# One level of Strassen's algorithm in the second MLP's first product

## The chip, the core and the metric

The kernel runs on one core of a Trainium2 chip, in one launch. The metric is the device time in microseconds (us): the median of three runs.

## The reference

Causal attention with a forget-gate decay over 4 batches of 8 heads (576 rows, head size 64) gives 2304 tokens of 512 features. Two MLPs of 2048 hidden units follow it, each one product into the hidden units, a leaky maximum and one product out of them. The change concerns the second MLP alone, above all its product `x @ w_in`.

```python
def _moe_ref(x, w_in, w_out):            # first MLP
    h = x @ w_in
    g = np.maximum(0.01 * h, h)
    return g @ w_out

def _moe2_ref(x, w_in, w_out, alpha):    # second MLP; alpha: one slope per hidden unit
    h = x @ w_in
    g = np.maximum(h, 0.0) + alpha * np.minimum(h, 0.0)
    return g @ w_out
```

## The kernel before

The engines are TensorE (PE), VectorE (DVE), ScalarE (ACT), GpSimd (POOL) and SyncE (SP), which issues every DMA. Each float32 operand of a big product is carried as two float32r parts, hi + lo, and a product is three matmuls: hi·hi, hi·lo and lo·hi. The tiles are 128 partitions high. A "chunk" is 128 hidden units, so an MLP has 16 chunks (`NF`); each chunk's weights come in two "halves" of 128x512, into the units (half 0) and out of them (half 1).

`Plan` is a list scheduler. Every operation is handed to it (`on`, `plan.op`) with the engine or engines that may take it, an expected time, a due time and the tiles that it touches. Each engine takes the operation that is due first among those whose operands and ring slots are there, and the operations are emitted in the order of these planned starts. So the order on each engine is fixed when the program is built, and at run time each engine goes through its list in order.

The stages lie one after the other:

- Attention of a group of queries (`attention_head`, `attention_scores`, `attention_weights`) is done beside the first MLP's block before the one that needs it.
- The first MLP works in nine blocks of 256 tokens (`T`). `moe_h` computes two chunks of hidden units into one PSUM bank: 2 x 4 x 3 = 24 matmuls with 256 columns. ACT and DVE make the leaky maximum into `gr` and split it into `g` (hi, lo). `moe1_y` adds 24 matmuls to the outputs of each block in two banks (`y`); the outputs go to DRAM (`yd`). 14 of its 32 halves are kept in DRAM once they are converted (`wscr`) and are loaded again in every block (`w_stream`, tiles `ws`); the others stay on chip (tiles `w`).
- The second MLP works in nine blocks of 256 tokens too. `moe2_x` loads a block from `yd` (tile `yraw`) and splits it into `x`. `moe_h` (line 522) makes the units, as before, with the slopes from `nalpha` (ACT lines 536 and 539, DVE line 546). `moe2_y` (line 642) multiplies them out: 6 matmuls with 512 columns per chunk, for two token tiles, added up in two banks.
- `weight` loads a half, which comes as float64, puts a float32 together from its words (one pass of ACT or POOL, three of DVE: lines 453 to 469) and splits it into hi and lo (lines 361 and 366, the helpers' lines `cast` and `sub`). The second MLP's 32 halves are converted from the last block of the first MLP on, and all of them stay on chip.

PSUM has eight banks: two (`y`) hold the blocks' outputs, six (`a`) take everything else.

The lines of a product into the units are

```python
for c in range(c0, c1):
    for i, (a, s) in enumerate(((0, 0), (0, 1), (1, 0))):
        pe.matmul(h()[:, f - f0], lhsT=w.ap[:, a, c * P : (c + 1) * P], rhs=x.ap[:, s, c], ...)
```

Of the kernel before, what the change touches and what calls it, by code (L numbers as in the profile page):

```python
# [19 lines left out]
P = 128  # L20
# [7 lines left out]
PARTS = ((0,), (1,))  # L28
CW = 512
NCV = 2  # L30
NRAW2 = 2
PSG = 0
# [4 lines left out]
NSTREAM = 14  # L37
# [6 lines left out]
NG = 2  # L44
NYSB = 2
W2LEAD = 0
# [16 lines left out]
class Buf:  # L63
    """One tile of a ring; it is allocated when its first operation is emitted."""
# [23 lines left out]
class Plan:  # L88
    """List scheduling: operations are given with engine, expected time, due
    time and the buffers they touch; each engine takes the one that is due  # L90
    first among those whose operands and slots are there. They are emitted in
    the order of their start."""
# [5 lines left out]
    def latency(a, b):  # L98
        """Expected time between the end of an operation and its user's start."""
# [27 lines left out]
    def run(self):  # L127
# [29 lines left out]
        def cost(o, eng, now):  # L157
            """When o would be done on an engine, with a price on the shared ports."""
# [9 lines left out]
        def better(o, eng, now):  # L168
            """Whether no other engine is a better place for o."""
# [13 lines left out]
        while events:  # L183
# [7 lines left out]
            for eng, queue in queues.items():  # L191
                if free.get(eng, 0) > now:
                    continue
                for n in [n for _, n in queue]:
# [17 lines left out]
                    if eng == "pe":  # L212
                        # the array's clock is halved after a tick with few columns
# [31 lines left out]
# Expected times in ns for n columns.  # L245
# [90 lines left out]
    # Due times in ns: the first MLP's blocks of T rows follow the prologue, and  # L336
    # each group's attention is due during the block before the one it belongs to.
# [789 lines left out]
```

## Time and profile before

| | |
|---|---|
| runs | 1044.31, 1044.84, 1046.48 us; median 1044.84 us |
| span of the profiled execution, first to last instruction | 1043.5 us |
| PE busy, matmuls | 1024.1 us, 7466 |
| DVE, ACT, POOL busy | 651.7, 603.6, 85.9 us |
| granted TensorE clock, mean | 0.997 |
| DMA | 166.50 MB, 160 GB/s |

The three runs stand for the time; the profiled execution is a further one, of which the profile shows the span alone. What lies around the span is taken as 1044.84 - 1043.5 = 1.3 us. A row of the profile names a line of the kernel, the engine, the operation and the tiles it writes and reads (out<-in, buffer numbers left out), then how often and how long. The seconds of a matmul's row overlap with its neighbours' (the engine is pipelined), so what a matmul costs is read from the starts of the pieces in the timeline and not from its duration.

### The profile page before, as it was taken

The numbers are of one execution on the slowest core, as the hardware profiler recorded it, in microseconds if no ns is written. First come the engines' busy times: TensorE is split into PE (matmuls) and PEld (weight loads), VectorE is DVE, ScalarE is ACT, GpSimd is POOL, SyncE is SP. The second block draws the span as 40 slices with busy tenths as digits, with TensorE's granted clock in tenths as the row PEclk, the third lists the DMA queues.
The fourth block names the chain that finished last, engine by engine and source line by source line (L and its number), as shares of the span: only waits on it lengthen the run. The fifth ranks groups of instructions, "written<-read, shape, count | busy, mean of one in ns | idle before, by whom it ended". The sixth has DMA issues, their size and how long they took to land.

```text
span 1043.5 us, 20123 instructions
## 1 busy us (share of the span) xinstructions
PE 1024.1 (98%) x7466; PEld 964.6 (92%) x7466; DVE 651.7 (62%) x1837; ACT 603.6 (58%) x1354; POOL 85.9 (8%) x159
## 2 busy tenths in 40 slices
PE   7899999999999999999999999999999999999998
PEld 5698999999999999999999999999999999999997
DVE  7799898888887877788885689423222322322322
ACT  7878787767787877887753456334333323323333
POOL 2000221210121111112010001000000000000000
PEclk9999999999999999999999999999999999999999
DMA  8899898576575665767489783001010100000000
GB/s 268 306 311 325 299 308 290 182 255 222 161 257 190 239 217 166 231 229 235 150 280 321 233 311 102 9 33 41 2 41 1 41 21 21 21 2 21 1 21 21
DMA packets 63234, 166.50 MB, mean 160 GB/s; under 512 B 6592, under 2 KB 20320, under 8 KB 63136
## 3 DMA queue, kind: packets, MB, share of 16 engines
q1 hardware_dynamic: 63136, 165.21, 47.2%
q8 instruction: 59, 0.97, 0.4%
q14 instruction: 39, 0.32, 0.1%
HBM read 148.29 MB, written 16.89 MB: 158 GB/s over the span
## 4 chain that ended last, share of the span: by engine, by line
PE 91%; DMA 6%; DVE 2%; ACT 1%; issue 0%; SPq 0%; ACTq 0%; DVEq 0%
PE bank L522 37%; PE bank L642 19%; PE bank L591 18%; PE bank L881 6%; PE bank L938 5%; PE bank L795 4%; PE bank L785 2%; DMA qk<-qk 2%; DMA vr<-v 1%; DMA ws<-wscr 1%; DMA yraw<-yd 1%; DMA raw<-w 1%; DVE g L366 0%; DVE t L895 0%; DVE cv L469 0%
## 5 line engine op out<-in xcount | busy, mean ns | idle before, releaser
L522 PE MATMUL bank<-x,w 128*128 128x256 f32 x1944 | 257.3, 284 | 0.1
L522 PEld LDWEIGHTS bank<-x,w 128*128 128x128 f32 x1944 | 243.7, 191 | 3.6 <-issue 0.4
L546 DVE SCALAR_TENSOR_TENSOR gr<-gr,nalpha,bank 128x256 f32<-128x256 f32 x144 | 62.8, 477 | 213.1 <-ACT bank L539 213.1
L361 ACT ACTIVATE g<-gr 128x512 fp32r<-128x512 f32 x143 | 90.1, 630 | 86.1 <-DVE gr L546 73.9
L366 DVE TENSOR_TENSOR g<-gr,g 128x512 fp32r<-128x512 f32 x144 | 100.6, 699 | 54.3 <-ACT g L361 53.9
L522 PE MATMUL bank<-x,ws 128*128 128x256 f32 x972 | 132.3, 285 | 1.2 <-DMA ws<-wscr 1.2
L536 ACT ACTIVATE gr<-bank 128x512 f32<-128x512 f32 x72 | 43.1, 598 | 154.7 <-PE bank L522 153.8
L642 PE MATMUL bank<-w,g 128*128 128x512 f32 x540 | 132.1, 391 | 0.0
L522 PEld LDWEIGHTS bank<-x,ws 128*128 128x128 f32 x972 | 123.5, 191 | 3.6 <-DMA ws<-wscr 1.7
L591 PE MATMUL bank<-g,ws 128*128 128x256 f32 x864 | 121.7, 288 | 1.3 <-ACT g L361 1.0
L591 PE MATMUL bank<-g,w 128*128 128x256 f32 x864 | 119.7, 286 | 0.0
L642 PEld LDWEIGHTS bank<-w,g 128*128 128x128 f32 x540 | 99.2, 188 | 19.4
L591 PEld LDWEIGHTS bank<-g,ws 128*128 128x128 f32 x864 | 109.5, 191 | 2.8 <-ACT g L361 1.4
L591 PEld LDWEIGHTS bank<-g,w 128*128 128x128 f32 x864 | 109.1, 191 | 0.4 <-issue 0.2
L906 ACT ACTIVATE t<-t,nm 128x128 f32<-128x128 f32 (+4 forms) x160 | 92.6, 580 | 17.2 <-DVE nm L895 16.6
L921 ACT ACTIVATE t<-t,nm 128x128 f32<-128x128 f32 (+4 forms) x139 | 78.2, 574 | 18.9 <-DVE nm L767 17.5
L858 POOL TENSOR_SCALAR_AFFINE_SELECT dm<-cb 128x128 f32<-128x128 f32 (+2 forms) x120 | 59.3, 496 | 358.3 <-DVE nm L895 274.9
L361 ACT ACTIVATE pt<-bank 128x128 fp32r<-128x128 f32 (+4 forms) x189 | 72.0, 408 | 25.9 <-PE bank L938 24.4
L938 PE MATMUL bank<-ident,t 128*128 128x128 f32 (+1 forms) x480 | 73.5, 269 | 1.5 <-ACT t L921 1.3
L952 DVE TENSOR_TENSOR pt<-bank,pt 128x128 fp32r<-128x128 f32 (+1 forms) x144 | 62.4, 452 | 11.7 <-ACT pt L361 10.3
L522 PE MATMUL bank<-x,v 128*128 128x256 f32 x540 | 69.6, 283 | 0.0
L522 PEld LDWEIGHTS bank<-x,v 128*128 128x128 f32 x540 | 68.1, 192 | 1.5
(98 smaller groups left out, 1407.6 us busy)
## 6 DMA issues: line engine op xcount, KB each, us to landing
ws<-wscr SPq DMA_DIRECT2D x112, 512.0 KB, 4.5
raw<-w SPq DMA_DIRECT2D x64, 512.0 KB, 6.3
qk<-qk SPq DMA_DIRECT2D x32, 416.0 KB, 4.4
qk<-qk SPq DMA_DIRECT2D x32, 320.0 KB, 4.5
cb<-cum_d SPq DMA_DIRECT2D x32, 288.0 KB, 4.4
vr<-v SPq DMA_DIRECT2D x16, 480.0 KB, 4.9
wscr<-ws SPq DMA_DIRECT2D x14, 512.0 KB, 5.7
cb<-cum_d SPq DMA_DIRECT2D x31, 160.0 KB, 4.2
```

The lines of the kernel that those rows point to most:

```text
L361: act.activation(out=out, in_=in_, func=AF.Copy)
L366: (dve if e == "dve" else gps).tensor_tensor(out=out, in0=in0, in1=in1, op=ALU.subtract)
L522: pe.matmul(h()[:, f - f0], lhsT=w.ap[:, a, c * P : (c + 1) * P], rhs=x.ap[:, s, c], start=c == 0 and i == 0, stop=c == NC - 1 and i == 2,)
L546: dve.scalar_tensor_tensor(out=gr.ap[:, i], in0=gr.ap[:, i], scalar=nalpha[:, f0 + i : f0 + i + 1], in1=h()[:, i], op0=ALU.mult, op1=ALU.add,)
L591: pe.matmul(acc[c // 2].ap[:, c % 2 * T :][:, :T], lhsT=w.ap[:, a, col : col + P], rhs=g.ap[:, s, at : at + T], start=f == 0 and (a, s) == ...
L642: pe.matmul(acc[t].ap, lhsT=g.ap[:, s, at + t * P : at + (t + 1) * P], rhs=w.ap[:, a], start=f == 0 and (a, s) == (0, 0), stop=f == NF - 1 ...
L858: gps.affine_select(out=dm.ap[:, : nk - split], in_=cb.ap[:, split:nk], pattern=[[-1, nk - split]], compare_op=ALU.is_ge, fill=-MASKED / S ...
L881: pe.matmul(sp_.ap[:, : s1 - s0], lhsT=q.ap[:, ql : ql + P], rhs=k, start=j == 0, stop=j == len(ks) - 1 and not masked,)
L906: act.activation(out=t.ap[:, :nk], in_=t.ap[:, :nk], func=AF.Exp, scale=-1.0, bias=nm.ap[:, last, u : u + 1], accum_out=nm.ap[:, 2, u : u ...
L921: act.activation(out=t.ap[:, :nk], in_=t.ap[:, :nk], func=AF.Copy, scale=nm.ap[:, 3, u : u + 1])
L938: pe.transpose(tp.ap[:, (j - j0) * nq : (j - j0 + 1) * nq], t.ap[p0:, k0 : k0 + P], ident[p0:, p0:])
L952: dve.tensor_tensor(out=lo, in0=src, in1=f32(hi), op=ALU.subtract)
```

## The change

The second MLP's product into the units is done by Strassen's algorithm (Winograd's form of it, 7 products and 15 sums), one level. The two by two blocks are: hidden units in two halves (chunk p and chunk p + 8, a "pair"), features in two halves of 256, tokens in two halves of 384 (`N2`). So the second MLP has three blocks of 768 tokens (`T2`) of eight pairs each.

- `weight2_in` converts both chunks' half 0 of a pair, forms the sums of weights (`comb`, four passes of 256 columns) and splits 3.5 tiles of 128x512 (`stage`), which go to DRAM (`w2in`). Pairs 2 to 5 are due during the first MLP's blocks 3 to 6 and are staged in tiles of the ring `g`, which now has three and is taken in any order; pairs 6, 7, 0 and 1 follow late in the first MLP. Pairs 0 and 1 stay on chip for the first block (tiles `wa`, `ws`); every other use loads the tiles from DRAM (`w2_stream`, up to 512 KB each).
- `moe2_x` loads 768 tokens in two parts (two of the four feature chunks each, tile `yraw`, of which there is one), forms four sums per part and splits seven operands.
- `moe2_h` does seven products per pair, each 6 matmuls with 384 columns into one bank of the ring `y`. ACT copies the first out, DVE adds the other six up in seven sums (`add`, line 720, reading PSUM) into four quarters, and makes the leaky maximum (lines 740 and 743) and the split of each quarter.
- `moe2_y` multiplies each quarter out: nine matmuls with 512 columns, into six banks of the ring `a`, which hold the block's outputs.
- The out halves (`weight2_out`) are converted from the end of the first MLP on, into the tiles `w` as they come free. The first MLP keeps 16 halves in DRAM instead of 14.

```diff
-NCV = 2
-NRAW2 = 2
+NCV = 3
-NSTREAM = 14
+NSTREAM = 16
-NG = 2
+NG = 3
...
+    T2 = 768
+    N2, NP, NB2 = T2 // 2, NF // 2, NT // T2
...
+        def stage(src, cols, k, n):
+            t = new(tag)
+            split_w(src, cols, t, d, n)
+            on("dma", t_dma(8 * n * P), d + 2e3, lambda: sp.dma_start(
+                out=w2in[p, k, :, :, :n], in_=f32(t.ap[:, :, :n])), r=[t], a=[(w2_b, (p, k))])
+            ts.append(t)
...
+        stage(v1, lambda: f32(v1.ap), 0, CW)
+        comb(s3, a11, a21, ALU.subtract, [v1, v2], [(sc, 0)])
+        comb(a21, a21, a22, ALU.add, [], [v2])
+        stage(v2, lambda: f32(v2.ap), 1, CW)
+        comb(s2, a21, a11, ALU.subtract, [v1, v2], [(sc, 1)])
+        stage(sc, lambda: flat(sc.ap), 2, CW)
+        comb(a12, a12, s2, ALU.subtract, [(sc, 1)], [v1])
+        stage(v1, a12, 3, h)
...
+    PRODUCTS = ((0, 0), (2, 1), (0, 1), (2, 0), (1, 0), (1, 1), (3, 0))
...
+        def product(k):
+            b = new("a" if early else "y")
+            t, o = ts[PRODUCTS[k][0]], PRODUCTS[k][1] * (CW // 2)
+
             def fn():
+                for c in range(2):
+                    for i, (a, s) in enumerate(((0, 0), (0, 1), (1, 0))):
                         pe.matmul(
+                            b.ap[:, :N2], lhsT=t.ap[:, a, o + c * P : o + (c + 1) * P], rhs=view(k)[:, s, c],
+                            start=c == 0 and i == 0, stop=c == 1 and i == 2,
                         )
...
+        p1, u2, u3, c22 = (new("r") for _ in range(4))
+        b = product(0)
+        on("act", t_act(N2) - 40, d - URGENT, lambda b=b: act.activation(out=p1.ap, in_=b.ap[:, :N2], func=AF.Copy), r=[b], w=[p1])
+        b = product(1)
+        add(1, u2, b, p1)
+        b = product(2)
+        add(2, p1, b, p1)
+        leaky(p1, 2, 0, 0)
...
+        b = product(6)
+        add(6, u2, b, u2)
+        leaky(u2, 6, 0, 1)
```

How the lists of two engines change is shown at two places. In the names, `x`, `bx` and `by` are the token operands, `wa` and `ws` the weight sums, `g` and `g2` the split units, `w`, `v` the halves of weights, `cv` and `raw` the conversion's tiles; the second number of a name only counts tiles.

PE in the middle of the second MLP, before: two chunks' products (line 522) and outputs (line 642).

```order
L522 MATMUL bank3_69<-x_1_9876,w9_1_0_8954 128x256 x12
L522 MATMUL bank3_69<-x_1_9876,ws_3_8963 128x256 x12
L522 MATMUL bank4_70<-x_1_9876,ws_1_9050 128x256 x6
L642 MATMUL bank0_66<-w7_0_0_8779,g_0_10877 128x512 x2
L642 MATMUL bank1_67<-w7_0_0_8779,g_0_10877 128x512 x2
L642 MATMUL bank0_66<-w7_0_0_8779,g_0_10877 128x512
```

PE at the same stage now, in the last block:

```order
L711 MATMUL bank0_69<-by_2_11293,ws_2_11904 128x384 x6
L780 MATMUL bank6_75<-w_8_9448,g2_0_12038 128x512 x2
L780 MATMUL bank4_73<-w_8_9448,g2_0_12038 128x512 x2
L780 MATMUL bank2_71<-w_8_9448,g2_0_12038 128x512 x2
L780 MATMUL bank6_75<-w_8_9448,g2_0_12038 128x512
L780 MATMUL bank4_73<-w_8_9448,g2_0_12038 128x512
L780 MATMUL bank2_71<-w_8_9448,g2_0_12038 128x512
L711 MATMUL bank1_70<-bx_3_10414,wa_0_11954 128x384 x6
L780 MATMUL bank5_74<-w_10_9571,g_1_12084 128x512 x2
L780 MATMUL bank3_72<-w_10_9571,g_1_12084 128x512 x2
L780 MATMUL bank7_76<-w_10_9571,g_1_12084 128x512 x2
L711 MATMUL bank0_69<-x_0_10479,wa_2_12011 128x384 x6
```

Blocks of 12 matmuls with 256 columns gave way to single products of 6 with 384, and between two of them stand six or nine matmuls of outputs; the units `g_1_12084` that are multiplied out behind line 711's second row come from the product in the first row.

PE where the first MLP ends, before (line 591 is its output, lines 522 and 642 are the second MLP's):

```order
L522 MATMUL bank3_69<-x_0_7973,v4_0_7823 128x256 x12
L591 MATMUL bank0_66<-g_1_9132,ws_2_8924 128x256 x4
L591 MATMUL bank1_67<-g_1_9132,ws_2_8924 128x256 x4
L591 MATMUL bank0_66<-g_1_9132,ws_2_8924 128x256 x2
L591 MATMUL bank1_67<-g_1_9132,ws_2_8924 128x256 x2
L591 MATMUL bank0_66<-g_1_9132,w15_1_0_1807 128x256 x4
```

PE there now (line 612 is the first MLP's output):

```order
L612 MATMUL bank0_69<-g_0_9222,w_15_1628 128x256 x2
L612 MATMUL bank1_70<-g_0_9222,w_15_1628 128x256 x2
L711 MATMUL bank4_73<-bx_0_8655,wa_0_8320 128x384 x6
L711 MATMUL bank3_72<-bx_2_8726,wa_0_8320 128x384 x6
L711 MATMUL bank2_71<-x_2_9191,wa_3_8443 128x384 x6
L711 MATMUL bank0_69<-bx_0_8655,ws_1_9133 128x384 x6
L711 MATMUL bank5_74<-bx_1_8717,wa_2_8433 128x384 x6
L711 MATMUL bank7_76<-bx_3_8735,wa_2_8433 128x384 x6
L711 MATMUL bank6_75<-x_0_8691,wa_1_8339 128x384 x6
L711 MATMUL bank4_73<-x_1_8779,wa_1_8339 128x384 x6
L711 MATMUL bank1_70<-bx_1_8717,ws_3_9219 128x384 x6
L780 MATMUL bank5_74<-w_0_8822,g_1_9377 128x512 x2
```

Before, products of the second MLP stood between the first's last outputs; now they stand behind all of them, nine products in a row.

DVE at that place, before (line 546 makes the second MLP's units, the other rows convert weights and split):

```order
L366 TENSOR_TENSOR g_1_9132<-gr_1_9089,g_1_9132 128x512
L463 SCALAR_TENSOR_TENSOR cv2_0_9015<-raw2_0_8965,cv2_0_9015 128x512
L546 SCALAR_TENSOR_TENSOR gr_0_9116<-gr_0_9116,nalpha_78,bank6_72 128x256 x2
L469 SCALAR_TENSOR_TENSOR cv2_0_9015<-raw2_0_8965,cv2_0_9015 128x512
L366 TENSOR_TENSOR g_0_9172<-gr_0_9116,g_0_9172 128x512
```

DVE there now (`yraw_0_9217` is the second part of the tokens):

```order
L382 TENSOR_TENSOR bx_0_8655<-yraw_0_9217,bx_0_8655 128x384
L382 TENSOR_TENSOR x_2_9191<-yraw_0_9217,x_2_9191 128x384
L382 TENSOR_TENSOR bx_2_8726<-yraw_0_9217,bx_2_8726 128x384
L382 TENSOR_TENSOR yraw_0_9217<-yraw_0_9217 128x384
L472 SCALAR_TENSOR_TENSOR cv_0_9224<-raw_3_9049,cv_0_9224 128x512
L382 TENSOR_TENSOR xt_0_9297<-yraw_0_9217 128x384
L382 TENSOR_TENSOR x_0_8691<-yraw_0_9217,x_0_8691 128x384
L382 TENSOR_TENSOR yraw_0_9217<-yraw_0_9217 128x384
L382 TENSOR_TENSOR bx_1_8717<-xt_0_9297,bx_1_8717 128x384
L382 TENSOR_TENSOR yraw_0_9217<-yraw_0_9217,xt_0_9297 128x384
L382 TENSOR_TENSOR bx_3_8735<-yraw_0_9217,bx_3_8735 128x384
L382 TENSOR_TENSOR w_6_9306<-cv_0_9224,w_6_9306 128x512
```

All of the second part's sums and splits now stand where PE wants the first products' operands, mixed with conversions.

## Rows read from the trace of the kernel before

**Rows 1.** The page: busy time, share of the span and instructions of each engine.

```profile
PE 1024.1 (98%) x7466; PEld 964.6 (92%) x7466; DVE 651.7 (62%) x1837; ACT 603.6 (58%) x1354; POOL 85.9 (8%) x159
```

**Rows 2.** The chain that ended last, shares of the span by line.

```profile
PE bank L522 37%; PE bank L642 19%; PE bank L591 18%; PE bank L881 6%; PE bank L938 5%; PE bank L795 4%; PE bank L785 2%; DMA qk<-qk 2%; DMA vr<-v 1%; DMA ws<-wscr 1%; DMA yraw<-yd 1%; DMA raw<-w 1%; DVE g L366 0%; DVE t L895 0%; DVE cv L469 0%
```

**Rows 3.** Stretches: length, each engine's busy time, granted clock, DMA share, GB/s.

```profile
25.00:170.00 145.00, 138.71 (x998) 126.84 (x998) 128.30 (x409) 115.94 (x291) 19.29 (x32) 1.00 0.91 310
170.00:450.00 280.00, 279.96 (x2305) 275.12 (x2302) 226.68 (x769) 214.27 (x533) 42.47 (x86) 1.00 0.66 217
450.00:520.00 70.00, 70.00 (x578) 69.28 (x579) 61.27 (x186) 55.97 (x127) 11.52 (x20) 1.00 0.58 197
...
590.00:660.00 70.00, 68.85 (x529) 66.50 (x528) 56.48 (x101) 38.02 (x67) 3.00 (x2) 1.00 0.56 195
660.00:1000.00 340.00, 340.00 (x2186) 310.68 (x2186) 104.11 (x201) 116.12 (x207) 0.00 (x0) 1.00 0.07 21
```

**Rows 4.** PE in order of time, from 916 us: start, length, line, operation, count.

```profile
916.30 5.20 PE L522 MATMUL bank<-x,w 128*128 128x256 f32 x42
921.34 1.55 PE L642 MATMUL bank<-v,g 128*128 128x512 f32 x6
922.72 1.52 PE L642 MATMUL bank<-w,g 128*128 128x512 f32 x6
924.08 0.88 PE L522 MATMUL bank<-x,w 128*128 128x256 f32 x6
924.80 2.91 PE L642 MATMUL bank<-w,g 128*128 128x512 f32 x12
927.54 2.68 PE L522 MATMUL bank<-x,w 128*128 128x256 f32 x21
```

**Rows 5.** PE's groups by shape: count, busy us, mean ns of one, idle before.

```profile
L642 PE MATMUL bank<-w,g 128*128 128x512 f32 x540 | 132.1, 391 | 0.0
...
L591 PE MATMUL bank<-g,w 128*128 128x256 f32 x864 | 119.7, 286 | 0.0
...
L881 PE MATMUL bank<-k 128*128 128x384 f32 x24 | 8.1, 338 | 0.0
```

**Rows 6.** What PE waited for: us in total, times, longest us.

```profile
PE bank L881 <- DMA qk<-qk: 7.3, 4, 4.4
...
PE bank L881 <- DVE nm L895: 1.0, 1, 1.0
PE bank L591 <- DVE g L366: 0.3, 1, 0.3
```

**Rows 7.** DVE in order of time at 471 us and 639 us, back to back.

```profile
470.76 0.68 DVE L366 TENSOR_TENSOR g<-gr,g 128x512 fp32r<-128x512 f32 x1
471.36 0.68 DVE L952 TENSOR_TENSOR pt<-bank,pt 128x512 fp32r<-128x512 f32 x1
471.96 0.60 DVE L895 CUSTOM_DVE_ANT_0 t<-bank,dm 128x448 f32<-128x448 f32 x1
...
639.01 0.75 DVE L460 TENSOR_SCALAR cv<-cv 128x512 int32<-128x512 int32 x2
```

**Rows 8.** All engines in order of time at the end of the span.

```profile
1033.71 0.59 ACT L539 ACTIVATE bank<-bank 128x512 f32<-128x512 f32 x1
...
1034.33 0.87 DVE L546 SCALAR_TENSOR_TENSOR gr<-gr,nalpha,bank 128x256 f32<-128x256 f32 x2 [0.56 <-ACT bank L539]
1035.30 0.63 ACT L361 ACTIVATE g<-gr 128x512 fp32r<-128x512 f32 x1 [1.00 <-DVE gr L546]
1035.96 0.69 DVE L366 TENSOR_TENSOR g<-gr,g 128x512 fp32r<-128x512 f32 x1 [0.76 <-ACT g L361]
...
1038.81 1.21 ACT L361 ACTIVATE ysb<-bank 128x256 f32<-128x256 f32 x4 [2.88 <-PE bank L642]
```

**Rows 9.** DMA issues: count, KB each, median us to landing.

```profile
ws<-wscr SPq DMA_DIRECT2D x112, 512.0 KB, 4.5
...
wscr<-ws SPq DMA_DIRECT2D x14, 512.0 KB, 5.7
...
yraw<-yd SPq DMA_DIRECT2D x9, 512.0 KB, 3.8
```

More of the change, by code (lines that the diff above doesn't have):

```diff
@@ L43 @@
 NGR = 2
-NG = 2
+NG = 3
 NYSB = 2
-W2LEAD = 0
+W2LEAD = 60e3
+NEARLY = 4
+W2FROM = 3
+W2EACH = 1
+W2LAG = 50e3
+W2STEP = 8e3
+W2OUT = 15e3
+AHEAD2 = 25e3
+NR = 8
+NG2 = 5
 NBC = 1
@@ L339, in tile_forgetting_attention_two_moe @@
     start, span, now = [], [], PROLOGUE
-    for i in range(2 * NB):
+    for i in range(NB):
         start.append(now)
@@ L420, in tile_forgetting_attention_two_moe @@
+    for b, ap in ((ident_b, ident), (warm_b, warm), (alpha_b, alpha), (cum_b, cum_d), (yd_b, yd), (wscr_b, wscr), (w2_b, w2in), (rate_b, rate), (tri_b, tri)):
         b.ap = ap
-    w_t = {}
-    def slot(which, f, half):
-        if which:
-            i = 2 * f + half
-            return f"v{i}" if i < NP2 else SLOTS2[i - NP2]
-        return "ws" if (f, half) in STREAM else f"w{f}_{half}"
-    SLOTS2 = [slot(0, *w) for w in HALVES if w not in STREAM[:-NSTR]]
-    NP2 = len(HALVES) - len(SLOTS2)
@@ L439, in weight, with assemble @@
-    def weight(which, f, halves, d):
-        n, at = 512 * len(halves), 512 * halves[0]
-        tag = "2" if which and f % 2 else ""
-        raw, v = new("raw" + tag), new("cv" + tag)
-        src = (w1, w2)[which].bitcast(I32)[f, :, 2 * at : 2 * (at + n)]
-        ts = [new(slot(which, f, half)) for half in halves]
+    w_t, w2_t = {}, {}
+    def assemble(which, f, half, d, after=()):
+        raw, v = new("raw"), new("cv")
+        src = (w1, w2)[which].bitcast(I32)[f, :, 2 * CW * half : 2 * CW * (half + 1)]
@@ L494, in w_stream @@
     def w_stream(f, half, d):
-        t = w_t[0, f, half] = new(slot(0, f, half))
+        t = w_t[0, f, half] = new("ws")
         on("dma", t_dma(4096 * P), d, lambda: sp.dma_start(out=f32(t.ap), in_=wscr[f, half]),
                 r=[(wscr_b, (f, half))], w=[t])
-    x_t = {}
+    x_t, begun = {}, {}
     URGENT = 8e3
@@ new lines, in product, with add, split, hi @@
+            on("pe", t_mm(N2, 6), d + k * step, fn, r=[t, bt[k]], w=[b], after=[begun[NB - 1, NF - 2]])
+            return b
+        def add(k, out, b, x):
+            on("dve", t_dve(N2), d + k * step - URGENT, lambda: dve.tensor_tensor(
+                out=out.ap, in0=b.ap[:, :N2], in1=x.ap, op=ALU.add), r=[b] if x is out else [b, x], w=[out])
+        def split(c, k, i, j):
+            g = new(("g", "g2", "g", "g")[2 * i + j])
+            u = d + k * step - URGENT
+            def hi(e):
+                cast(e, g.ap[:, 0, :N2], c.ap)
+            def lo(e):
+                sub(e, g.ap[:, 1, :N2], c.ap, f32(g.ap[:, 0, :N2]))
+            plan.op(t_cast(N2), u, hi, r=[c], w=[(g, "hi")], shared=True)
+            plan.op(t_sub(N2), u, lo, r=[c, (g, "hi")], w=[(g, "lo")], shared=True)
+            gs[i, j] = g
@@ new lines, in moe2_h @@
+        gs = {}
+        p1, u2, u3, c22 = (new("r") for _ in range(4))
[6 more added lines that the diff above has]
+        leaky(p1, 2, 0, 0)
+        b = product(3)
+        add(3, u3, b, u2)
+        b = product(4)
+        add(4, c22, b, u3)
+        add(4, u2, b, u2)
+        leaky(c22, 4, 1, 1)
@@ new lines, in moe2_h, with moe2_y, mm, fn @@
+        b = product(5)
+        add(5, u3, b, u3)
+        leaky(u3, 5, 1, 0)
+        b = product(6)
+        add(6, u2, b, u2)
+        leaky(u2, 6, 0, 1)
+        return gs
+    def moe2_y(bi, p, ts, gs, acc):
+        t0, d = bi * T2, due2(bi, p + 1)
+        quarters = ((0, 0), (1, 1), (1, 0), (0, 1))
+        for k, (i, j) in enumerate(quarters):
+            w, g = w_t[1, p + NP * i, 1], gs[i, j]
+            for t in range(N2 // P):
+                def mm(s, t=t, i=i, j=j, w=w, g=g):
+                    def fn():
+                        for a in range(2 - s):
+                            pe.matmul(
+                                acc[j * (N2 // P) + t].ap, lhsT=g.ap[:, s, t * P : (t + 1) * P], rhs=w.ap[:, a],
+                                start=p == 0 and i == j and (a, s) == (0, 0), stop=p == NP - 1 and i != j and s == 1,
+                            )
+                    return fn
+                at = d + PAIR / 14 * (2 * k + 1 if p < NP - 1 else 7 + j * (N2 // P) + t)
+                on("pe", t_mm(512, 2), at, mm(0), r=[w, (g, "hi")], w=[acc[j * (N2 // P) + t]])
+                on("pe", t_mm(512), at + 1, mm(1), r=[w, (g, "lo")], w=[acc[j * (N2 // P) + t]])
+        if p == NP - 1:
+            halves = 2 if bi == NB2 - 1 else 1
+            m = DM // halves
+            for t in range(T2 // P):
@@ L1028, in tile_forgetting_attention_two_moe @@
     for f in range(NF):
-        for halves in PARTS:
-            weight(0, f, halves, due(0, f) - 10e3 + 1e3 * halves[0])
+        for half in range(2):
+            weight1(f, half, due(0, f) - 10e3 + 1e3 * half)
     for bi in range(NB):
@@ L1057, in tile_forgetting_attention_two_moe, with reopen, fn @@
-    ring("cv2", NRAW2, [P, CW], I32, pool="p2", after=opened)
-    d0, d1 = start[NB - 1] - W2LEAD, start[NB] + 0.3 * span[NB]
-    for f in range(NF):
-        for halves in PARTS:
-            weight(1, f, halves, d0 + (d1 - d0) * (2 * f + halves[0]) / len(HALVES))
-    for bi in range(NB, 2 * NB):
-        moe2_x(bi)
-        acc = [new("y") for _ in range(T // P)]
-        for f in range(0, NF, 2):
-            g = moe_h(bi, f)
-            for i in range(2):
-                moe2_y(bi, f + i, g, acc)
+    def reopen(ctx2, name, side):
+        def fn():
+            ctx2.close()
+            pools[name] = ctx.enter_context(tc.tile_pool(name=name, bufs=1, side=side))
+        return fn
```

249 lines of the change are left out of this document (149 added, 100 removed).

## The prediction

> **What bounds the kernel now.** I read the busy shares first: PE is at work for 1024.1 of 1043.5 us and no other engine for more than 62% [rows 1]. The chain that ended last is mostly three lines of matmuls, the second MLP's 522 and 642 among them [rows 2]. Then I cut the span into its stages. From 660 to 1000 us, the second MLP alone, PE is busy in 340.00 of 340 us at full clock, DVE in 31% and ACT in 34%, and DMA is nearly idle [rows 3]. From 170 to 520 us, the first MLP with attention beside it, PE is full too, but DVE is at 81 to 88% [rows 3]. So matmul time taken out of the second MLP comes out of the end one for one, as long as DVE, which takes over the sums, keeps up; and work that is moved ahead goes to a stage with little DVE time left.
>
> **Price of a matmul.** Six pieces of the steady stage give it by their starts [rows 4]: 42 matmuls with 256 columns from 916.30 to 921.34, 0.120 us each; 12 with 512 columns from 924.80 to 927.54, 0.228 us each. The difference is 0.42 ns per column, and 12 ns of each matmul do not depend on its width. No long run of 384 columns stands in the trace. In a line between the two it costs 0.174 us. In favour of the line: the durations of single ones, 286 ns at 256 columns, 338 at 384 and 391 at 512, lie on one [rows 5]. Ends: 0.180 (the rate of 256 columns) and 0.171 (the rate of 512).
>
> **Removed and added on PE.** Before: 9 blocks x 16 chunks x 12 = 1728 matmuls with 256 columns, 207.4 us. After: 3 blocks x 8 pairs x 7 products x 6 = 1008 with 384 columns, 175.4 us. That is 32.0 us less: 23 us from an eighth of the columns, 9 us from 720 fewer fixed parts. With the ends of the price: 26 to 35 us less. The outputs keep their 864 matmuls with 512 columns. A pair now takes 42 x 0.174 + 36 x 0.228 = 15.5 us of PE.
>
> The Trainium skill (TensorE: Matmul & The Clock Gate, section Back-to-back issue gap) gives a lone matmul's gap as the columns at 2.4 GHz plus about 2.5 ns, which would make 109 and 163 ns and, as an estimate, a gain of 24.9 us. The measured 120 and 228 ns do not agree with it, and the sum goes by them.
>
> **What DVE takes over.** Back to back, a 512-column pass with two operands takes 0.60 us, start to start [rows 7]; two passes of 256 take 0.87 [rows 8], so 384 columns lie between 0.44 and 0.60, and I take 0.52. A pass with one operand took 0.75 for two of 512 [rows 7], some 0.27 for 384. A pair needs seven sums, four halves of a maximum at 0.52 and four at 0.27, four lo parts: 3.6 + 3.2 + 2.1 = 8.9 us, beside 15.5 us of PE. In the mean that is hidden. ACT loses the two passes per bank (lines 536, 539) and gets five short ones; it is freer than before.
>
> What could fail is the delay. Between the product that completes the first quarter and the matmuls that use it the order puts one product and nine matmuls of outputs: 1.04 + 9 x 0.228 = 3.1 us. The chain there is sum, minimum, maximum, hi part: 0.52 + 0.27 + 0.52 + 0.5 = 1.8 us, with four hand-overs of 0.03 to 0.1 us as at the end of the span [rows 8], so 2.2 us. 0.9 us are left for another pass that is ahead on DVE, and such a pass is 0.5 us. I take no loss in the steady stage.
>
> **The first MLP's stage.** A pair's sums of weights cost DVE two conversions (0.38 + 0.60 + 0.60 each), three and a half lo parts and four sums of 256 columns: 3.2 + 2.2 + 1.7 = 7.1 us. Four pairs are moved into four blocks of about 70 us, in which DVE was busy for 57 and, in the last, 61 us [rows 3]: now 64 to 68 of 70. A stage of that kind stands in the trace: from 25 to 170 us DVE is busy 88%, and PE stands for 6.3 of 145 us; but most of this is waiting for loads of q and k, and DVE is named for 1.0 us [rows 6]. So the ends are 0 (450 to 520 us, 88% and no idle time) and 4.3% of 280 us, 12 us. Add to it the staging. Each staged tile is stored before its slot is free, a store of this size lands after 5.7 us [rows 9], and at 14 of the 24 staged tiles of pairs 2 to 7 the next writer of the slot stands only 3 to 5 us of PE behind the store; ACT, which casts, then stands for a microsecond or two with everything behind it. PE has a bank or two of work ahead, so I take 5 us for the whole stage, nearer to 450-520 us, and 0 to 14 as ends. Two more halves in DRAM are two more loads of 4.5 us landing per block [rows 9], 10 us ahead: nothing.
>
> **Where the MLPs meet.** Before, products of the second MLP filled the first's last gaps, and PE stood for 1.15 us between 590 and 660 [rows 3]. Now the first MLP's last outputs wait for their own units, whose chain has conversions in it: 0.6 us. Then come nine products (9.4 us), and DVE must split the second part of the tokens for them, which cannot be loaded before the first part has left the one tile `yraw`. The order has 30 DVE passes from the last units' maximum to the first quarter's: ten of 0.60, two of 0.38, sixteen of 0.52, one of 0.44, one of 0.27, together 15.8 us, begun some 2.2 us before PE ends the outputs of the units before the last. PE needs 2.9 + 9.4 = 12.3 us in that stretch. DVE ends at 13.6, the cast adds 0.5, so 1.8 us are lost; the load is half as large again as the one that lands in 3.8 us [rows 9] and costs about 0.8 more. Conversions of the out halves (2.2 us each, two per pair) fill DVE to 13.3 of 15.5 us per pair through this block; I add 1.3 us. Together 4.5 us, less the 1.15 that stood there: 3.4 us, ends 0 and 9.
>
> **Block changes and end.** Twice the next block's tokens are split in the last pair's time, with `yraw` again loaded in sequence: 0.5 us each, 1 us, ends 0 and 4. Streaming 3.5 tiles per pair is 1.8 MB in 15.5 us, 118 GB/s, where 310 GB/s were moved from 25 to 170 us [rows 3], and each tile is loaded a pair ahead: hidden; uncovered, a tile would cost its 4.5 us. After the last matmul, four copies and a store remain as before [rows 8]: nothing.
>
> **The sum.** Span 1043.5 - 32.0 + 5 + 3.4 + 1 = 1020.9; with 1.3 us around it, as the median stands to the span, 1022 us. The ends of the terms that are likely together give 1015 to 1028.
>
> **Rivals.**
>
> *Little is lost:* the order covers the conversions and the meeting as well as 450 to 520 us were covered. Then 1044.8 - 32 and 0 to 2 us: 1013. For it: PE had no idle time at 88% DVE [rows 3]. Against: the nine products in a row.
>
> *The first MLP's stage is crowded:* DVE full and ACT behind the staging stores cost 12 to 16 us instead of 5: 1029 to 1033. For it: 97% DVE in the last of these blocks. Against: PE's rows name DVE for 1.3 us in the whole span [rows 6].
>
> *The quarters come late:* every pair has four gates, a quarter's chain against the matmuls that use it, 96 in all, and PE goes through its list in order. If DVE's list puts passes of a neighbouring quarter ahead, the 0.9 us of room are gone, and each tenth of a microsecond of lateness costs 9.6 us. From 0.27 us per gate on the kernel is slower than before; at 0.35 it takes 1022 + 34 = 1056 us. For it: seven dependent sums per pair, where before one chain per two chunks had six banks of room, and now two banks. Against: 57% DVE, and an engine that falls behind by one pass catches up in the next gap.
>
> *The wider matmul saves no fixed part:* 384 columns cost 0.180 us, gain 26 us: 1028. The page of the skill named above would give a gain of this size (24.9 us, 1029).
>
> *The change doesn't do what it says:* the weights' tiles come late from DRAM, because SP's list is in order and a load behind a store that waits for its tile waits too. 22 pairs at 0.6 us each would give 13 us: 1035.
>
> **How the numbers follow.** Forecast (1015 to 1028) 0.62; crowded stage 0.14; little lost 0.10; late quarters 0.05; no fixed part saved 0.03; late tiles 0.03; more than one of these 0.03. The predicted time is 1022 us. The range 1011 to 1033 holds the forecast, little lost, no fixed part saved and most of the crowded stage, 0.86; I keep it, since the prices of the delays are estimates. A measurement of this kernel can tell 0.2%, 2.1 us, from no change. Slower by more needs late quarters at their price: 0.05. Within 0.2%: 0.02. Faster: 0.93.
>
> **What would show it.** Products of 6 matmuls 1.04 us apart from start to start (1.08: the fixed part). DVE at 55 to 60% in the second MLP, and PE there without idle time; if PE is named waiting for `g` on ACT or DVE in each pair, the quarters are late. From 270 to 490 us PE idle 2 to 8 us, ACT waiting for DMA on `g`. Where line 711 begins, PE idle 3 to 6 us, released by ACT or DVE rows on `bx`, `x` and `g`. I am wrong if PE is at less than 97% from 650 us on.

## The result, and the profile after

The changed kernel takes 1032.5 us (median of 4 runs, 1028.8 to 1037.2), the kernel before in the same comparison 1044.6 (1043.6 to 1046.5): ratio 0.9875, interval 0.9839 to 0.9911. It is 12.0 us faster, where 22.6 were forecast. The profiled execution has a span of 1029.6 us and took 1031.4, so 1.8 us lie around the span and not the 1.3 that were taken from two different executions.

First the busy shares, then the stretches of [rows 3] (columns: PE, weight loads, DVE, ACT, POOL, granted clock, DMA share, GB/s):

```profile
PE 999.5 (97%) x6746; PEld 936.6 (91%) x6746; DVE 794.3 (77%) x2166; ACT 565.6 (55%) x1311; POOL 82.1 (8%) x156
```

```profile
25.00:170.00 145.00, 133.02 (x912) 120.15 (x913) 119.51 (x368) 108.05 (x264) 13.41 (x23) 0.96 0.83 284
170.00:450.00 280.00, 277.88 (x2279) 272.47 (x2280) 237.75 (x795) 217.16 (x539) 50.16 (x93) 1.00 0.76 254
450.00:520.00 70.00, 69.30 (x566) 67.88 (x565) 63.51 (x199) 58.48 (x136) 12.85 (x23) 1.00 0.88 298
590.00:660.00 70.00, 67.73 (x528) 66.43 (x527) 54.42 (x102) 34.89 (x64) 0.00 (x0) 1.00 0.92 314
660.00:1000.00 340.00, 340.00 (x1697) 306.85 (x1696) 241.17 (x499) 84.13 (x163) 1.02 (x1) 1.00 0.42 138
```

The last row is the stage the change is about: PE full, DVE at 71% instead of 31%. The four rows above it are stages in which time was to be lost. The least expected is the first: PE is busy for 133.0 of the 145 us in which it was busy for 138.7 before, and the granted clock fell to 0.96.

PE in order of time where the MLPs meet (start, length, line, operation, count; in brackets idle time and what ended it):

```profile
644.62 1.70 PE L612 MATMUL bank<-g,ws 128*128 128x256 f32 x12 [1.24 <-ACT g L377]
...
648.64 1.66 PE L711 MATMUL bank<-bx,wa 128*128 128x384 f32 x8 [0.19 <-DVE bx L382]
...
652.22 2.24 PE L711 MATMUL bank<-bx,wa 128*128 128x384 f32 x12
654.30 2.24 PE L711 MATMUL bank<-x,wa 128*128 128x384 f32 x12
...
658.37 1.89 PE L780 MATMUL bank<-w,g 128*128 128x512 f32 x7 [0.78 <-ACT g L377]
```

12 matmuls with 384 columns lie between 652.22 and 654.30: 0.173 us each, a product 1.04 us. The three waits sum to 2.2 us. The passes that DVE took over, in the same stretch (back to back, so the cost is start to start):

```profile
651.47 0.55 DVE L382 TENSOR_TENSOR yraw<-yraw 128x384 f32<-128x384 f32 x1
651.94 0.55 DVE L382 TENSOR_TENSOR bx<-xt,bx 128x384 fp32r<-128x384 f32 x1
...
658.14 0.41 DVE L740 TENSOR_SCALAR gr<-r,alpha 128x384 f32<-128x384 f32 x1
658.47 0.56 DVE L720 TENSOR_TENSOR r<-bank,r 128x384 f32<-128x384 f32 x1
658.93 0.56 DVE L382 TENSOR_TENSOR g<-r,g 128x384 fp32r<-128x384 f32 x1
```

A sum of 384 columns takes 0.47 us, from on-chip memory or from PSUM, and a pass with one operand 0.33.

What PE waited for in the first 170 us (us in total, times, longest):

```profile
PE bank L925 <- DMA vr<-v: 5.8, 2, 3.1
PE bank L1021 <- DMA qk<-qk: 4.9, 2, 4.2
PE bank L1078 <- ACT t L1061: 3.4, 5, 1.6
PE bank L564 <- DMA ws<-wscr: 2.8, 1, 2.8
```

Beside [rows 6], the loads of `v` cost more, and a streamed half of weights is waited for, which did not occur before. The row of `v` in the same stretch of the kernel before:

```profile
PE bank L785 <- DMA vr<-v: 2.5, 3, 1.4
```

### The profile page after: what moved, and what is told of

Same layout as the page of the kernel before. It is cut to its first block, busy times and chain, and to the rows that moved or that the text cites. A ratio compares the mean times of both kernels' runs of the same rounds, so it can differ in the third digit from the quotient of the medians.

```text
span 1029.6 us, 19383 instructions
## 1 busy us (share of the span) xinstructions
PE 999.5 (97%) x6746; PEld 936.6 (91%) x6746; DVE 794.3 (77%) x2166; ACT 565.6 (55%) x1311; POOL 82.1 (8%) x156
## 4 chain that ended last, share of the span: by engine, by line
PE 81%; DMA 10%; DVE 5%; ACT 2%; issue 1%; SPq 0%; ACTq 0%; DVEq 0%
PE bank L780 19%; PE bank L612 16%; PE bank L711 16%; PE bank L564 16%; PE bank L1021 4%; PE bank L1078 4%; DMA raw<-w 4%; PE bank L935 3%; DMA vr<-v 3%; PE bank L925 2%; DMA ws<-wscr 2%; DMA w2in<-g 1%; DVE cv L467 1%; DVE t L1035 1%; DVE cv L472 0%
## 5 line engine op out<-in xcount | busy, mean ns | idle before, releaser
L780 PE MATMUL bank<-w,g 128*128 128x512 f32 x864 | 223.3, 392 | 0.8 <-ACT g L377 0.8
L780 PEld LDWEIGHTS bank<-w,g 128*128 128x128 f32 x864 | 160.2, 188 | 24.3 <-ACT g L377 1.1
L720 DVE TENSOR_TENSOR r<-bank,r 128x384 f32<-128x384 f32 x168 | 91.2, 555 | 77.9 <-PE bank L711 77.2
L564 PE MATMUL bank<-x,w 128*128 128x256 f32 x972 | 136.6, 287 | 0.5 <-ACT x L377 0.3
L564 PEld LDWEIGHTS bank<-x,w 128*128 128x128 f32 x972 | 123.6, 191 | 2.1 <-DVE x L382 0.6
L1046 ACT ACTIVATE t<-t,nm 128x128 f32<-128x128 f32 (+4 forms) x160 | 92.5, 579 | 16.2 <-DVE nm L1035 15.4
L1061 ACT ACTIVATE t<-t,nm 128x448 f32<-128x448 f32 (+4 forms) x140 | 79.2, 577 | 15.8 <-DVE nm L907 14.1
L377 ACT ACTIVATE pt<-bank 128x128 fp32r<-128x128 f32 (+5 forms) x190 | 72.4, 407 | 22.8 <-PE bank L1078 21.4
L382 DVE TENSOR_TENSOR g<-r,g 128x384 fp32r<-128x384 f32 x96 | 53.9, 561 | 22.1 <-ACT g L377 22.1
L1078 PEld LDWEIGHTS bank<-ident,t 128*128 128x128 f32 (+1 forms) x480 | 52.9, 142 | 13.7 <-ACT t L1061 7.1
```

The lines of the kernel that those rows point to most:

```text
L377: act.activation(out=out, in_=in_, func=AF.Copy)
L382: (dve if e == "dve" else gps).tensor_tensor(out=out, in0=in0, in1=in1, op=ALU.subtract)
L720: on("dve", t_dve(N2), d + k * step - URGENT, lambda: dve.tensor_tensor(out=out.ap, in0=b.ap[:, :N2], in1=x.ap, op=ALU.add), r=[b] if x is ...
L780: pe.matmul(acc[j * (N2 // P) + t].ap, lhsT=g.ap[:, s, t * P : (t + 1) * P], rhs=w.ap[:, a], start=p == 0 and i == j and (a, s) == (0, 0), ...
L1046: act.activation(out=t.ap[:, :nk], in_=t.ap[:, :nk], func=AF.Exp, scale=-1.0, bias=nm.ap[:, last, u : u + 1], accum_out=nm.ap[:, 2, u : u ...
L1061: act.activation(out=t.ap[:, :nk], in_=t.ap[:, :nk], func=AF.Copy, scale=nm.ap[:, 3, u : u + 1])
```

## The experiments

Four theories for the missing 10 us; A to C have the letters that the expectations give them. **A**: the choice of the streamed halves. With 16 halves of the first MLP in DRAM instead of 14, block 1 needs halves into the units early, and PE waits for their loads. **B**: the conversions that were moved into blocks 3 to 6 cost more than 5 us. **C**: any new setting, the three tiles `cv` for conversions instead of two (`NCV`) too, gives the first two blocks another order, in which loads come late by chance. **D**: the second MLP does not gain what was forecast, for instance because each quarter is late.

All kernels are in one table; busy and span are of the profiled execution, idle is their difference, "first 170" is PE's busy time there. A single execution lies up to 6.4 us off the median of its kernel's runs, and the kernel before took 1044.6 to 1045.7 us beside the different groups of runs, so sizes go by the ratios and places by the spans.

| kernel | us | ratio to before, interval | span | PE busy | idle | first 170 |
|---|---|---|---|---|---|---|
| before | 1044.6 | | 1043.5 | 1024.1 | 19.4 | 157.7 |
| before, 15 halves | 1048.3 | 1.0038 [1.0022, 1.0053] | 1047.2 | 1026.6 | 20.6 | 157.5 |
| before, 16 halves | 1051.7 | 1.0056 [1.0034, 1.0078] | 1051.2 | 1027.2 | 24.0 | 155.6 |
| before, 18 halves | 1050.7 | 1.0054 [1.0038, 1.0071] | 1051.7 | 1026.5 | 25.2 | 152.7 |
| before, 16 halves, NCV 3 | 1057.5 | 1.0123 [1.0105, 1.0140] | 1055.7 | 1030.6 | 25.1 | 152.4 |
| **changed** | 1032.5 | 0.9875 [0.9839, 0.9911] | 1029.6 | 999.5 | 30.1 | 150.8 |
| changed, out halves streamed | 1032.8 | 0.9861 [0.9837, 0.9886] | 1030.4 | 1003.1 | 27.3 | 155.0 |
| changed, no early pairs | 1042.0 | 0.9964 [0.9942, 0.9985] | 1039.3 | 1004.9 | 34.4 | 153.2 |
| changed, NCV 2 | 1028.8 | 0.9815 [0.9786, 0.9843] | 1023.4 | 998.0 | 25.4 | 156.5 |
| changed, four loads | 1032.2 | 0.9872 [0.9854, 0.9890] | 1028.4 | 999.9 | 28.5 | 150.9 |
| changed, dear quarters (one run) | 1033.2 | | 1031.4 | 1001.5 | 29.9 | 151.7 |
| changed, NCV 2, four loads | 1020.0 | 0.9769 [0.9744, 0.9794] | 1016.4 | 995.4 | 21.0 | 157.0 |
| changed, NCV 2, four loads, out halves | 1018.3 | 0.9737 [0.9709, 0.9766] | 1016.2 | 995.9 | 20.3 | 157.6 |

### 16 halves in the kernel before

```diff
-NSTREAM = 14
+NSTREAM = 16
```

> The kernel before, with 16 of the first MLP's halves kept in DRAM instead of 14, picked as the changed kernel picks them; nothing else. In the changed kernel PE was busy 150.8 us of the first 170, before 157.7, and lost some 3 us more at half clock. Theory A (the loss is made by which halves are streamed: with 16, halves into the units are among the first that block 1 needs, and PE waits for them): 1049 to 1055 us, about 5 to 10 more than before, with PE waiting for ws from wscr at the start of the second block. Theory B (the loss is made by the conversions that were moved into blocks 3 to 6): 1043 to 1047, as before. Theory C (any new setting makes the planner order the first two blocks anew, and how late SP's loads come there is chance): anywhere from 1040 to 1052, with waits on loads of q, k, v in the first 170 us, not on ws above all.

It costs some 6 us, and the products have nothing to do with it. PE's row for the first 170 us, of the kernel before and of this one (PE busy, granted clock, DMA share, GB/s):

```profile
0.00:170.00 170.00, 157.70 (x1078) 0.99 0.90 304
```

```profile
0.00:170.00 170.00, 155.62 (x1050) 0.99 0.90 304
```

Of the 4.6 us more of idle time 2.1 lie here; the rest is spread up to 590 us. No streamed half is waited for in the first 170 us; what is longer than before are waits for ACT and for loads of `v`. The time lies in the ranges of A and of C, the missing wait speaks for C, and B, which expected no change here, does not explain these 6 us.

### 16 other halves in the changed kernel

```diff
-    STREAM = [HALVES[1 + i * (len(HALVES) - 4) // (NSTREAM - 1)] for i in range(NSTREAM)]
+    STREAM = [(f, 1) for f in range(NF)]
```

> The changed kernel, with the 16 halves out of the units streamed and all halves into them kept on chip. Theory A: the wait of 2.8 us on ws near 137 us and the stretch at half clock behind it go: 1024 to 1028 us. Theory B: 1030 to 1036, no change. Theory C: the first two blocks are ordered anew, 1022 to 1037.

The total stays, where A expected 1024 to 1028 us. The wait on `ws` is gone, the first 170 us gain 4 us of PE and 170 to 520 us 2. But where the MLPs meet PE now loses 4.7 us in two waits for ACT, and the same matmuls are busy for 3.6 us more in sum:

```profile
645.35 2.80 PE L711 MATMUL bank<-bx,wa 128*128 128x384 f32 x9 [2.93 <-ACT bx L377]
658.20 2.34 PE L780 MATMUL bank<-w,g 128*128 128x512 f32 x9 [1.75 <-ACT g L377]
```

So the same number of halves can be streamed at a smaller price in the first blocks, A alone does not explain the total, and the order at the meeting depends on settings that do not name it.

### No pairs converted early

```diff
-NEARLY = 4
+NEARLY = 0
```

> The changed kernel, with no pair's sums of weights moved into the first MLP's blocks 3 to 6 (all but two of the eight pairs are staged late in the first MLP, in the tiles wa). Theory A and C: idle time of PE from 170 to 520 us falls from 2.8 to below 1 us, the conversions crowd the last block of the first MLP instead (2 to 6 us of idle time more there): 1030 to 1036. Theory B: 1020 to 1026.

PE is busy for 350.00 of 350 us from 170 to 520 us instead of 347.18, so the moved conversions cost 2.8 us there, and the kernel is 9.5 us slower, 6 us more than A and C expected at most. All eight pairs now crowd the meeting: from 590 to 720 us PE is idle for 10.5 us instead of 2.3, in part in waits for the conversions' results:

```profile
658.45 0.50 PE L780 MATMUL bank<-w,g 128*128 128x512 f32 x1 [3.44 <-ACT w L377]
...
667.23 6.46 PE L780 MATMUL bank<-w,g 128*128 128x512 f32 x27 [1.55 <-ACT g L377]
```

Theory B falls: the moved work costs about 3 us where it is put, and more where it came from.

### Two tiles for conversions

```diff
-NCV = 3
+NCV = 2
```

> The changed kernel, with two of the conversion's tiles cv instead of three, as before. Theory A: the streamed halves are the same, so the first 170 us lose as much, PE busy 150 to 152 us of them: 1030 to 1036. Theory B: the same. Theory C: PE busy in the first 170 us differs by several us either way, 1024 to 1038, with no relation to ws.

6.3 us faster by the ratios (3.7 in the medians, 6.2 in the spans); PE is at work for 156.5 of the first 170 us, at a granted clock of 1.00. The streamed halves are the same 16, so A, which expected 150 to 152 of 170, falls as the whole cause, and C holds. But the meeting is worse:

```profile
633.51 2.37 PE L612 MATMUL bank<-g,ws 128*128 128x256 f32 x12 [2.49 <-ACT g L377]
650.09 3.21 PE L780 MATMUL bank<-w,g 128*128 128x512 f32 x9 [2.58 <-ACT g L377]
```

### 15 and 18 halves in the kernel before

```diff
-NSTREAM = 14
+NSTREAM = 15   # and 18 in the other
```

> The kernel before with 15 halves of weights streamed through DRAM instead of 14. If each half more costs by itself (a store and a load more, a wait on its load), half of what the run with 16 cost is expected: 1047 to 1049 us against 1045, with waits on streamed halves in the first 170 us or in 170 to 450. If what the run with 16 showed was another order of the first two blocks, the time goes with no rule by the number: anywhere from 1042 to 1052, the loss or gain lies ahead of 170 us, and no wait on a streamed half stands there.

> The kernel before with 18 halves streamed instead of 14. If each half more costs by itself, twice what 16 cost: 1056 to 1060 us. If it is the order of the first two blocks that changes with any setting, 1043 to 1053 without a rise over the run with 16, and TensorE's busy time ahead of 170 us (157.7 before) explains the difference.

1048.3 and 1050.7 us. By the ratios, 15, 16 and 18 halves cost 4.0, 5.9 and 5.6 us: up with the first half more, and from there on the intervals overlap. The run with 15 is where a fixed price per half put it (and in the wide range of order alone), the run with 18 is 5 us below that price and where order alone put it. With 15 the first 170 us are as before, against what order alone led me to expect, and 520 to 590 us lose 1.7; with 18 the first 170 us lose 5.0. So there is no fixed price for a half, and no one place at which it is paid. That each kernel has an order of its own is certain (before and with 15 halves the lists of PE part at the 462nd matmul, with 16 or 18 at the 126th); that the order is what costs, and not the traffic, these two don't show.

### The token part loaded early, with two and with three tiles

The second part of the first 768 tokens is no longer loaded through the one tile `yraw`, late, but in four quarters into the four tiles `r`, which are not needed before the second MLP. The DVE passes are the same.

```diff
-            raw, e2 = new("yraw"), new("xt")
+            e2 = new("xt")
+            if bi == 0 and c == 1:
+                raws = [new("r") for _ in range(4)]
...
+                            sp.dma_start(out=r.ap, in_=yd[:, 2 * i + c, t0 + j * N2 : t0 + (j + 1) * N2])
...
+                q11, q12, q21, q22 = (lambda r=r: r.ap for r in raws)
```

> The changed kernel with two staging tiles for conversions (NCV 2, the run of 1028.8), and in it the second part of the second MLP's first token block read early in four quarters into four tiles instead of late through the one tile yraw. If the stall where the MLPs meet is the wait for yraw and for the splits of that part, the idle time of TensorE between 590 and 720 us falls from about 5 us to 3 or less and the time to 1023 to 1027. If the conversions of the last weights or the last units' chain set it, nothing changes there, and the time stays at 1027 to 1031.

1020.0 us, 3 us better than expected. PE stands still nowhere between 590 and 720 us; the stretch 590 to 660 with two tiles for conversions, without and with the four loads:

```profile
590.00:660.00 70.00, 64.93 (x461) 0.95 0.73 250
```

```profile
590.00:660.00 70.00, 70.00 (x508) 1.00 0.79 270
```

5.1 us of idle time and the clock's fall with them were worth 7.0 us of span and 4.8 by the ratios (8.9 in the medians, of two groups of runs). Whether the earlier load itself does it, or the order that the plan makes with it, is not told apart.

> The changed kernel as it is (three staging tiles for conversions), with only the early load of the second token part in four quarters into four tiles. TensorE's order is word for word that of the changed kernel until late in the first MLP, so the first 170 us are the same. If that start is the term that was mis-sized, it costs here too what it costs the changed kernel: TensorE busy for 150 to 152 of the first 170 us, the meeting (590 to 720 us) without idle time, and 1027 to 1031 us in all. If the meeting alone made the difference to 1020, this kernel takes 1019 to 1023.

With three tiles the same edit gains next to nothing: 1032.2 against 1032.5, a microsecond above the range expected. The meeting is clean (129.91 of 130 us), the start is that of the changed kernel (150.93 and 150.84), and 1.5 us that the meeting gave are idle between 520 and 590 us instead. So NCV alone, 3 against 2, is worth 10.8 us by the ratios in this pair of kernels (12.2 in the medians, 12.0 in the spans).

### Dear quarters

```diff
-            plan.op(t_sub(N2), u, lo, r=[c, (g, "hi")], w=[(g, "lo")], shared=True)
+            for _ in range(2):
+                plan.op(t_sub(N2), u, lo, r=[c, (g, "hi")], w=[(g, "lo")], shared=True)
```

> The changed kernel with the second pass that makes each quarter of a unit (the remainder of the split into two parts) done twice, some 2 us more of VectorE for each pair of products. By the theory that the steady stage has room for the quarters: TensorE stays full from 660 us on, VectorE rises from 65 to about 79 of 100 us in 800 to 900, and the time stays at 1031 to 1036 (what the first stage may lose by another order within it). If the quarters were just in time, each pair would lose up to 2 us: 1050 or more.

1033.2 us in one run. The stretch 800 to 900 us, PE, weight loads, DVE, ACT, POOL:

```profile
800.00:900.00 100.00, 100.00 (x500) 90.23 (x499) 74.74 (x155) 20.65 (x41) 0.00 (x0) 1.00 0.39 119
```

DVE rose from 65.5 to 74.7 of 100 us, less than the 79 expected, and PE did not notice. D falls, as far as late quarters go: the second MLP has room for more passes than it was given.

### Both settings in the kernel before

```diff
-NCV = 2
+NCV = 3
-NSTREAM = 14
+NSTREAM = 16
```

> The kernel before with 16 halves in DRAM and three staging tiles for conversions instead of two, which are the two settings of the change that reach the first MLP's first blocks. With 16 halves alone it took 1051.7 us, TensorE busy for 155.6 of the first 170 us. If three staging tiles are what spoils the start, 1055 to 1060 us and 150 to 153 of 170. If each setting merely gives another order of the first blocks, anything between 1044 and 1058, and the difference to the run with 16 stands in the first 170 us.

1057.5 us: the change's two settings without its algorithm cost 12.9 us (11.0 to 14.6 by the interval), and the total and the first 170 us lie where they were expected if three tiles spoil the start; the wider range of mere order, 1044 to 1058, holds the total too. This is the missing time. PE's rows for 0 to 170 us here, and for 0 to 100 us before and here:

```profile
0.00:170.00 170.00, 152.41 (x987) 0.96 0.88 302
```

```profile
0.00:100.00 100.00, 89.28 (x548) 0.98 0.89 299
0.00:100.00 100.00, 86.96 (x505) 0.95 0.88 298
```

At 170 us PE is 91 matmuls behind the kernel before (987 against 1078). At the 2305 in 280 us of [rows 3] that is an estimated 11 us, and from there to the end PE is idle for 7.5 us, 7.1 before. So nearly the whole loss is made by 170 us. Of the 91, 43 are missing at 100 us already, where no streamed half is waited for. Of these, 25 are lost from 25 to 37.5 us (before, then here), behind a load of `v`, with the granted clock at 0.59:

```profile
25.00:37.50 12.50, 9.74 (x60) 1.00 0.85 277
25.00:37.50 12.50, 9.96 (x35) 0.59 0.68 238
```

```profile
27.93 2.37 PE L785 MATMUL bank<-pt,vr 128*128 128x320 f32 x6 [2.54 <-DMA vr<-v]
```

In the other part stands a stall near 137 us. The lists of PE in this kernel and in the changed one agree in shapes and tiles for the first 810 matmuls, and so does this stall. PE's gaps around 130 us here, with the ten matmuls behind the last:

```profile
132.83 0.41 PE L881 MATMUL bank<-k,k 128*128 128x320 f32 x1 [0.92 <-DVE nm L895]
135.76 0.33 PE L938 MATMUL bank<-ident,t 128*128 128x128 f32 x1 [0.44 <-DVE nm L895]
139.29 1.14 PE L522 MATMUL bank<-x,ws 128*128 128x256 f32 x6 [3.20 <-ACT g L361]
140.23 3.62 PE L785 MATMUL bank<-pt,vr 128*128 128x256 f32 x10
```

and in the changed kernel:

```profile
131.44 0.42 PE L1021 MATMUL bank<-k,k 128*128 128x320 f32 x1 [0.92 <-DVE nm L1035]
134.37 0.33 PE L1078 MATMUL bank<-ident,t 128*128 128x128 f32 x1 [0.44 <-DVE nm L1035]
137.51 1.62 PE L564 MATMUL bank<-x,ws 128*128 128x256 f32 x6 [2.81 <-DMA ws<-wscr]
138.93 4.04 PE L925 MATMUL bank<-pt,vr 128*128 128x256 f32 x10
```

The gaps are the same two and then one of some 3 us at the first matmul of block 1 with a streamed half; the profile names ACT's pass as what came last in the one kernel, the load in the other. It is the load in both. Here the third of the loads of `ws` is issued at 132.23 and lands 6.9 us later, at 139.13, just ahead of the matmul. And the same pass of ACT ends in the changed kernel at 137.64, when this matmul has already begun, so it does not need that pass (the load here, the pass there):

```profile
ws<-wscr SPq DMA_DIRECT2D x1, 512.0 KB, 6.9
```

```profile
137.01 0.63 ACT L377 ACTIVATE g<-gr 128x512 fp32r<-128x512 f32 x1 [0.76 <-DVE gr L578]
```

So the price of the two settings together is shown. This stall is a wait for a streamed half, as A has it, but it hangs on the order, as C has it: the same 16 halves with NCV 2 do not have it.

### The two together with the out halves

The kernel of 1020.0 us with the `STREAM` line of the second experiment.

> The kernel of 1020.0 us (two staging tiles, four loads), with the 16 streamed halves chosen as all the halves out of the units instead of every second half of both kinds. If the waits of the start come from streaming halves into the units early, the first 170 us gain up to 5 us: TensorE busy for 158 or more, 1014 to 1018 us. If it is the order alone that decides, there is no rule: 1016 to 1027, and the meeting stays at 2 us of idle time or less.

1018.3 us, the first 170 us at 157.6, just short of what was expected if early halves into the units make the waits (158 and 1014 to 1018), and in the range of order alone; the meeting has 0.8 us of idle time. Its runs and the other's overlap (1014.9 to 1019.9 and 1018.2 to 1024.4), so that it is the better one is likely and not certain; that both beat the changed kernel, by 11 us or more by the ratios, is.

## Why the prediction was right on the side and short on the size

**What bounds the kernel: right.** PE without idle time and at full clock from 660 to 1000 us, as forecast; the 31.1 us by which PE's busy sum fell (next paragraph) came out of the span, less 5.0 us of idle time in other stages.

**Price and number of the products: right.** 0.173 us against the 0.174 of the line through two widths, so 720 fixed parts were saved and the rival that saved none falls. The formula for a lone matmul's gap (the Trainium skill, TensorE: Matmul & The Clock Gate, Back-to-back issue gap) makes an estimate of 163 ns for this width; the trace's 173 ns do not agree with it. The whole of the change can now be measured with the two settings held equal: the kernel before with 16 halves and NCV 3 against the changed one. PE's busy sum falls from 1030.6 to 999.5, 31.1 us (forecast 32.0), its idle time rises from 25.1 to 30.1, 5.0 us (forecast 9.4: 5 + 3.4 + 1), and the times differ by 25.9 us by the ratios, 25.0 in the medians (forecast 22.6). So without the two settings' price the change gains more than was forecast.

**DVE's passes: right to a tenth of a microsecond; DVE's share: too low.** 0.47 us for a sum taken as 0.52, 0.33 for a pass taken as 0.27, back to back. The forecast share was 55 to 60%, and the trace shows 65.5 of 100 us from 800 to 900 and 71% from 660 to 1000. A pass that does not lie back to back with the next counts with its whole record, 0.56 or 0.42 us: up to 15 x 0.56 + 4 x 0.42 = 10.1 us per pair instead of 8.9. And the next block's tokens are split in these stretches too. The late quarters did not occur, and stayed away with a pass more in each quarter.

**The first MLP's stage: right place, half the size.** Forecast 5 us, 0 to 14; from 170 to 520 us PE is idle for 2.8, in waits for ACT and DVE, and the run without early pairs is idle for 0 there. The staging stores had hardly a part in it: ACT waits on one for 1.1 us, once. DVE went to 63.5 of 70 us in 450 to 520, where 64 to 68 were forecast for a block of 70 us. The crowded stage of the rivals gives 1029 to 1033, and the measured 1032.5 lies in it, but not by its mechanism: its 12 to 16 us are not in these blocks. That the stated range, 1011 to 1033, holds the result is luck: it reached that far for this rival, and what filled it stood in no term.

**The meeting: right place, a third of the size.** 2.3 us idle from 590 to 660 instead of 1.15, so +1.1 for the forecast 3.4. That the size hangs on the order is shown by the two neighbours: 5.1 us with NCV 2, 5.8 with other halves. The edit that loads the second token part early removes these waits, with two tiles (70.00 of 70) and with three (69.91). The block changes, forecast at 1 us, cost nothing (340.00 of 340 us).

**The step that failed:** "Two more halves in DRAM are two more loads of 4.5 us landing per block [rows 9], 10 us ahead: nothing", together with NCV, which the diff showed and the sum gave no term. Both are priced by one run: 12.9 us instead of 0. The premise was wrong in the trace too. In the chain that ended last of the changed kernel, from 130 us on (start, length):

```profile
130.56 6.82 DMA ws<-wscr
137.38 0.14 issue
137.51 1.62 PE bank L564 x6
```

PE came to this half at 134.70 (137.51 less 2.81). The load was issued 4 us before that, not 10, and took 6.8 us, not 4.5: the median of [rows 9] is that of loads in all blocks, and those of block 1 run beside the attention's loads. What differs is the lead: with 16 halves and NCV 2 in the kernel before, such loads take 5.6 to 7.5 us there too, and PE waits for none.

Where the 12.9 us lie: in the spans 12.2, of which 5.7 are idle time of PE (19.4 to 25.1), and 6.5 a longer busy time of the same 7466 matmuls, most of it at a lower granted clock (a mean of 0.993 against 0.997, 4 of 1055 us). In the changed kernel the rows behind the stall show it (PE, weight loads, DVE, ACT, POOL, clock, DMA share, GB/s):

```profile
139.00:141.00 2.00, 2.00 (x6) 1.61 (x6) 0.00 (x0) 0.00 (x0) 0.00 (x0) 0.50 0.00 0
143.00:145.00 2.00, 2.00 (x18) 1.87 (x16) 1.02 (x4) 0.89 (x4) 0.00 (x0) 0.98 0.44 127
```

**What stays open.** Why this order of the first blocks is the worse one is not settled. Halves and NCV were priced together and one by one (16 alone 6 us; NCV 3 on top some 7 more by the ratios; NCV 3 alone does not fit on chip beside 14 halves, so no run has it). They act by the list that the plan makes from them: by shapes and tiles, the lists with 16 halves and NCV 2, before and changed, agree for 857 matmuls, those with NCV 3 for 810, and these two families differ from the 126th matmul on (all counted in the order of the starts). In the five kernels with NCV 3 and this choice of halves PE stands for 2.2 to 3.5 us at the first streamed half; in the three with 16 such halves and NCV 2 it does not. But no run moved this load, or the loads of `v`, alone: which of them starts the loss was not isolated.

## What to carry over

A change often brings settings with it that make its memory fit: price each of them as an edit of its own, in the stage it touches, even if the change is about another stage, and have the old kernel with the new settings measured as the baseline. Here the list scheduler turned the size of one ring into another order from the 126th matmul on, so a term of nothing for such a setting needs a look at the first place where the two lists part. And a median landing time from a whole span is no price for a load in the most crowded stage.

## What was not expected of the hardware

A short stall of PE can cost more than its length. Ten matmuls with 256 columns of one line take 2.11 us in the kernel before, and 4.04 in the changed one right behind the gap of 2.8 us at 137.51, where the granted clock is 0.50, the lower of its two levels (1.2 GHz), from 137.5 to 143 us (rows above):

```profile
108.83 2.11 PE L785 MATMUL bank<-pt,vr 128*128 128x256 f32 x10
```

Not each stall has this price. In the same kernel PE stands for 2.64 us until 38.95 us, waiting for `v`, and the clock stays at the upper level (2.4 GHz) behind it:

```profile
39.00:41.00 2.00, 2.00 (x13) 1.61 (x14) 0.53 (x1) 0.44 (x2) 0.00 (x0) 1.00 0.96 313
```

Summed over the kernel the price is half as much as the idle time: against the kernel with NCV 2 and four loads, the changed one has 9.1 us more of idle time, and 4.1 us more of busy time for the same 6746 matmuls; its mean granted clock, 0.994 against 0.999, would account for 5 of 1030 us.
